# A four-layer transformer kernel on one core: the Fourier layer's residual tiles move to other homes and another queue, and the next layer's first weights are split earlier

## The chip, the core and the metric

The kernel runs on one core of a Trainium2 chip. A core has a matrix engine (PE, with its weight loads shown apart as PEld), a vector engine (DVE), an engine for functions of one input (ACT), a general engine (POOL) and a queue engine (SP) that mostly issues transfers. Each engine works through its own instructions in order and waits on semaphores of the others. Transfers between the chip's memory (HBM) and the on-core memory (SBUF) run on 16 DMA engines. They are issued here from two places: SP, whose transfers the profile lists as queue q1 ("hardware_dynamic"), and POOL, whose transfers are queue q0 ("software_dynamic").

The metric is the time of one execution in microseconds, as a median of several runs.

## What is computed

Four layers on x, a 2048 x 640 matrix of float32: attention, Fourier, attention, Fourier. Each is added to its input.

```python
def _A_ref(x, wqkv, wo):            # 32 heads of 20
    q, k, v = split((x @ wqkv))
    p = softmax(q k^T / sqrt(20))
    return (p @ v) @ wo

def _B_ref(x, dft_seq_re, dft_seq_im, dft_hid_re, dft_hid_im):
    a = x @ dft_hid_re^T
    b = x @ dft_hid_im^T
    return dft_seq_re @ a - dft_seq_im @ b

x = x + _A_ref(_layernorm(x), A_wqkv, A_wo)
x = x + _B_ref(_layernorm(x), ...)
x = x + _A_ref(_layernorm(x), A_wqkv, A_wo)
x = x + _B_ref(_layernorm(x), ...)
```

## The kernel before

The program has two equal halves, each of one attention layer and one Fourier layer. The first half writes its result to a buffer in HBM, `d_x[1]`; the second half reads it and writes the output.

**An attention layer** starts with a prologue (`prologue`, from line 284). For each of four blocks of 512 rows, PE turns the normalized rows (`turn`, tiles `xa` to `ptr`, split by ACT and DVE into two parts `xt`), makes the first 128 columns of the queries and of the keys (`pqk`, two times 15 matmuls with the weights `w[0]` and `w[1]`) and half of the values (`pv`, 60 matmuls). A float32 matrix is handled as the sum of a rounded part and a rest: ACT casts (line 114) and DVE subtracts (line 115). That is `split`; `weights` is a split of a weight tile `wraw` into `wqk`. The attention proper follows (`psc`, `e`, `acc`), then the projection with `wo` (`py`, class `Project`), which adds the residual, writes the sum to `d_x[0]` (line 960) and normalizes it into the tiles `xn`.

**A Fourier layer** (`Fourier.run`, line 1224) uses the symmetry of the transform: the rows are folded, so that row blocks are handled in eight pairs t = 0 to 7, pair t being blocks t and t + 8. Its main loop has 16 steps; step i handles block m = `ORDER[i]` of the sequence matrix. In a step PE adds 9 matmuls to the sums `pacc` (`accumulate`); after the last of a group of four steps ACT and DVE split the sums into the tiles `u` (`turn`), which frees the banks of PSUM that hold them; and `parts(i + 6)` splits the matrix block that is needed six steps later (`craw` to `chl`) and, after the second block of a pair, issues the load of a further 512 KB piece of the matrix into the freed `craw` slot (line 1119, on SP). The last three such loads are issued at steps 0, 1 and 3.

From step 11 on, `hidden(t)` makes pair t: 18 matmuls `phid`, one ACT copy and two DVE operations that make the sum and the difference `r` (lines 1190 to 1192), then the residual is added: DVE adds the lower block, POOL the upper (lines 1200 and 1201), two instructions each, and SP stores the tile `xd` to `d_x[1]` or to the output (line 1222). `hidden(0)` to `hidden(3)` run within the main loop; `hidden(4)` to `hidden(7)` after it.

**The residual tile** of a pair is 640 KB, loaded from `d_x[0]` by `residual(t)` (line 1197) on POOL's queue. Its home is one of six tiles `x0` to `x5` in the pool `own`. Pairs 0 to 3 are asked for at steps 2, 3, 5 and 7, pairs 4 and 5 at steps 8 and 9. Pairs 6 and 7 reuse the homes of pairs 0 and 1 and are asked for just ahead of `hidden(4)` and `hidden(5)`; since POOL also adds the upper blocks, these two requests stand between its additions.

**The passage to the next half.** `after(s)`, called ahead of `hidden(4)`, makes a `Start` of the next attention layer: ACT normalizes its first 512 rows out of the residual tiles of pairs 0 to 3, and SP asks for `wraw` and for `wvraw`. After `hidden(7)` and the release of the pools the prologue opens a pool `pro`, whose tiles `w0` and `w1` take the split weights, and loads rows 512 to 1023 (`xa`), which are the lower blocks of pairs 4 to 7.

The addresses follow from the pools. In the kernel before, the tile for `w[0]` lies on the addresses of the tile that is home to pairs 1 and 7.

```python
        def residual(s, t):
            s.x[t] = s.own(f"x{t % 6}", [2, D], F32, "xd")
            G.dma_start(s.x[t], pair(s.src, t))
```

Of the kernel before, what the change touches and what calls it, by code (L numbers as in the profile page):

```python
# [19 lines left out]
ND = D // 128  # L20
# [15 lines left out]
def mha_fnet_kernel(ctx, tc, x_in, wqk, wv, wo, seq, hid, nat_seq, nat_hid, out):  # L36
# [123 lines left out]
    class Qkv:  # L160
# [98 lines left out]
            else:  # L259
                A.activation(dst, src, AF.Copy)  # L260

        def begin(s, first, kq, vals, given):


            s.first, s.given = first, given
            for k in range(2):
                if given:
                    s.xn[k] = first(f"x{k}", [2, D], F32, "xa")
                    for i in range(2):
                        normed(s.xn[k][:, i], given.x[2 * k + i][:, 0], given.next[k], i)  # L270
                else:
                    s.load(k)
            s.fetch(0, kq, "k3")
            s.fetch(ND, kq, "k4")
            s.wvraw = [vals(f"v{NT - 1 - dc}", [HD], F32, "wvraw") for dc in range(ND)]
            if given:
                s.load_values()
# [2 lines left out]
            for dc in range(ND):  # L280
                nc.sync.dma_start(s.wvraw[dc], wv[dc, :, :HD])

        def prologue(s, vals, xt, fill, room, att):
            s.xtp, s.fill, s.room = xt, fill, room
            for k in (2, 3):
                s.load(k)
            if not s.given:
                s.load_values()
            s.top = const.tile([128, 2, ND, NB], F32, name="top", bufs=2)
            V.memset(s.top, 0.0)  # L290
            w = [room(f"w{k}", [2, ND, 128], F32R, "wqk") for k in range(2)]
            def values():
                s.wv = fill("wv", [ND, 2, HD], F32R, "wv")
                for dc in range(ND):
                    split(s.wv[:, dc, 0], s.wv[:, dc, 1], s.wvraw[dc])

            if s.given:
                s.weights(w[0], 0, False)
                s.turn(0)
                s.weights(w[1], ND, False)  # L300
                values()
            else:
                s.stats(0)
                s.norm(0)
                s.stats(1)
                for k in range(2):
                    s.weights(w[k], k * ND, False)
                s.norm(1)
                s.stats(2)
                s.turn(0)  # L310
                s.norm(2)
                s.stats(3)
                values()

            def ones(t):
                s.v[t] = vals(f"v{t}", [H * VW + 12], F32, "v")
                G.memset(s.v[t][:, :H * VW].rearrange("p (a c) -> p a c", c=VW)[:, :, DH:], 1.0)
                G.memset(s.v[t][:, H * VW:], 1.0)

            for t in range(NT - ND):  # L320
                ones(t)
            def later(tb, k, f):
                if tb + 2 < NB:
                    f(2 * tb + 4 + k)

            def own(tb, n):
                t = 4 * tb + n
                p = s.bank([128, HD], "pv")
                for dc in range(ND):
                    for f in s.value(p, t, dc):  # L330
                        f()
                s.own(p, t, 0, False)

            for tb in range(NB):

                sq, late = [], s.given and tb == 0
                for k in range(2):
                    later(tb, k, s.load)
                for k in range(2):
                    p = s.bank([128, 512], "pqk")  # L340
                    for dc in range(ND):
                        for f in s.product(p, w[k], tb, dc):
                            f()
                    sq.append(s.keep(p, k * ND, tb, False, (room, fill)[k]))
                    if late:
                        s.stats(2 + k)
                        continue
                    if tb == k == 0:
                        s.norm(3)
                    later(tb, k, s.stats)  # L350
                if late:
                    for n in range(4):
                        own(tb, n)
                        if n < 2:
                            s.norm(2 + n)
                            later(tb, n, s.stats)
                if tb == 0:
                    att.setup()
                elif tb == 1:
                    for t in range(NT - ND, NT):  # L360
                        ones(t)
                if tb + 1 < NB:
                    s.turn(tb + 1)
                for k in range(2):
                    later(tb, k, s.norm)
                    s.norms(s.bank([H, 512], "pn"), k * ND, tb, sq[k])
                if tb == 0:
                    att.qload(0, 0, None)
                elif tb == 1:
                    s.fetch(ND + 1)  # L370
                    for j in range(2):
                        att.kload(0, 0, j)
                elif tb == 2:
                    s.w1 = s.weights(s.fill("w", [2, ND, 128], F32R, "wqk"), ND + 1, True)
                    s.fetch(1)
                elif tb == NB - 1:
                    att.zeros(room)
                    list(s.bound(0, room))
                    att.qshift(0, 0)
                    for j in range(2):  # L380
                        att.kload(0, 1, j)
                if not late:
                    for n in range(4):
                        own(tb, n)
            s.made |= {0, ND}
# [656 lines left out]
    class Fourier:  # L1042
# [68 lines left out]
        ORDER = (0, 1, 4, 5, 2, 6, 3, 7) + tuple(range(8, 16))  # L1111
        AHEAD = 6

        def load(s, slot):

            if s.loads:
                n = s.loads.pop(0)
                s.raw[n] = s.keep(f"raw{slot}", [2, 512], F32, "craw"), slot
                nc.sync.dma_start(s.raw[n][0], seq[n // 4, n // 2 % 2, FIRST[n % 2 * 2] // 2])
# [73 lines left out]
            return r  # L1193

        def residual(s, t):
            s.x[t] = s.own(f"x{t % 6}", [2, D], F32, "xd")
            G.dma_start(s.x[t], pair(s.src, t))

        def add(s, e, x, r, r_mirror):
            e.tensor_tensor(x[:, :HD + 1], x[:, :HD + 1], r[:, :HD + 1], op=OP.add)  # L1200
# [2 lines left out]
        def hidden(s, t):  # L1203
# [8 lines left out]
            r = s.difference_and_sum(p, s.own(f"r{t % 2}", [3 * (HD + 2)], F32, "r"), 128)  # L1212
            if t in (0, 2):

                m = s.own("xs", [D], F32, "xs")[0:1]
                G.tensor_copy(m, hi[0:1])
                s.add(G, m, s.ym[:, t // 2], s.ym[:, 1 - t // 2])
            s.add(V, lo, r[:, 0], r[:, 1])
            s.add(G, hi, r[:, 1], r[:, 0])
            if t in (0, 2):  # L1220
                G.tensor_copy(hi[0:1], m)
# [2 lines left out]
        def run(s, after):  # L1224

            s.x, s.acc, s.nb, s.next = {}, {}, 0, {}
            for i, m in enumerate(s.ORDER):
                tb, ri, q = m // 8, (m // 4) % 2, m % 4
                s.accumulate(m)
                if q == NQ - 1:  # L1230
                    s.turn(tb, ri)
                s.parts(i + s.AHEAD)
                if m in (6, 7, 9, 10):
                    s.middle((6, 7, 9, 10).index(m))
                if 11 <= m < 14:
                    s.hidden(m - 11)
                if m == 13:
                    s.hidden(3)
                if m in (12, 13) and s.dst is not out:
                    k = m - 12  # L1240
                    s.next[k] = moments([s.x[2 * k + i][:, 0] for i in range(2)], 2, "a")
                if ri == 1 and m < 8:
                    s.residual(q)
                elif m in (8, 9):
                    s.residual(m - 4)
            s.keep.close()
            after(s)
            for t in range(4, NP):
                if t < 6:
                    s.residual(t + 2)  # L1250
                s.hidden(t)

        def general(s):

# [47 lines left out]
    class Start:  # L1302


        def __init__(s, L, src, general, given=None):
            s.tag = tag = f"{L}g" if general else f"{L}"
            s.q = Qkv(tag, src)
            s.q.flag = near[:, 5 + L:6 + L] if general else near[:, L:L + 1]
            s.a = Attention(s.q, tag)
            s.vals, s.a.kq, s.first = Pool(f"v{tag}"), Pool(f"kq{tag}"), Pool(f"first{tag}")  # L1310
            s.q.begin(s.first, s.a.kq, s.vals, given)

    def layer(start, src, dst, general, tasks, after):

# [2 lines left out]
        f = Fourier(p, d_x[0], dst, check)  # L1317
        f.tag = tag
        xt, fill = Pool(f"xt{tag}", "right"), Pool(f"fill{tag}", "right")
        room = Pool(f"pro{tag}")  # L1320
        banks(f"q{tag}")
        q.prologue(vals, xt, fill, room, a)
        room.close()
        start.first.close()

        room = a.room = check.room = Pool(f"att{tag}")
# [40 lines left out]
    def layers(general):  # L1367
        todo = [Start(0, x_in, general)]
        for L in range(LAYERS):
            last = L == LAYERS - 1  # L1370

            def after(f=None):
                if not last:
                    todo.append(Start(L + 1, d_x[1], general, f))

            layer(todo[L], d_x[1] if L else x_in, out if last else d_x[1], general, tasks[L], after)
            if general:
# [78 lines left out]
```

## Time and profile before

| | |
|---|---|
| time, median of 3 runs | 2580.6 us (2579.59 to 2583.07) |
| time of the profiled execution | 2582.69 us |
| its span, first to last instruction | 2580.8 us |
| PE busy | 2521.1 us, 98% |
| ACT busy | 2136.0 us, 83% |
| DVE busy | 981.2 us, 38% |
| POOL busy | 538.4 us, 21% |
| mean granted PE clock | 0.993 |
| first half's Fourier layer and passage, from the first `pacc` to the second half's first `pqk` at full pace | 1214.80 to 1298.65 us |
| second half's Fourier layer, from the first `pacc` to the last addition | 2497.42 to 2573.72 us |

The profiled execution is 2.1 us above the median of the runs and within their range. Its time is 1.9 us longer than its span. Shares over the whole span hide the Fourier layers, which are some 160 us of 2580; they have to be read with views cut to a stretch of time.

### The profile page before, as it was taken

The page shows a single profiled execution, that of the slowest core. Times are in us where ns is not written, and L with a number is a line of the kernel's source. Part 1 is how long each engine was busy: PE and PEld are TensorE (multiplying, and loading weights), DVE is VectorE, ACT ScalarE, POOL GpSimd, SP SyncE. Part 2 cuts the span into 40 slices and gives each one's busy share as a digit, 9 for nine tenths or more (in the row PEclk, how much of TensorE's full clock was granted, in tenths as well). Part 3 has the DMA queues.
Part 4 walks back from the last instruction along what each step waited for, and adds up shares of the span by engine and source line. Part 5 has one row for each costly group of instructions (what it writes and reads, how often), then busy time and mean ns, then how long its engine had stood idle before and what let it go on. Part 6 is the DMA issues. An engine that isn't in the chain of part 4 may idle for free.

```text
span 2580.8 us, 43627 instructions
## 1 busy us (share of the span) xinstructions
PE 2521.1 (98%) x16350; PEld 1161.6 (45%) x16350; DVE 981.2 (38%) x2081; ACT 2136.0 (83%) x2429; POOL 538.4 (21%) x1068
## 2 busy tenths in 40 slices
PE   8999999999999999999989999999999999999997
PEld 7644444443333332249775444444433333322596
DVE  5244422244232334317653444223332323332275
ACT  5688899988999999975356888999899999999752
POOL 2112111112111212114321211111111111121243
PEclk9999999999999999999999999999999999999998
DMA  5223221222322223336442332222221212133463
GB/s 175 95 91 122 83 86 44 85 88 85 94 70 87 87 81 109 123 96 236 181 164 93 105 119 89 66 65 72 84 83 51 80 51 77 52 94 97 131 245 130
DMA packets 124345, 262.53 MB, mean 102 GB/s; under 512 B 28016, under 2 KB 52368, under 8 KB 124124
## 3 DMA queue, kind: packets, MB, share of 16 engines
q1 hardware_dynamic: 83228, 149.30, 17.9%
q0 software_dynamic: 40896, 110.34, 13.5%
q8 instruction: 132, 2.16, 0.4%
q14 instruction: 89, 0.73, 0.1%
HBM read 175.29 MB, written 84.21 MB: 101 GB/s over the span
## 4 chain that ended last, share of the span: by engine, by line
PE 90%; DVE 4%; DMA 2%; POOL 1%; issue 1%; ACT 1%; DVEq 0%; SPq 0%; ACTq 0%; POOLq 0%
PE acc L534 37%; PE psc L523 27%; PE pqk L127 11%; PE pv L127 6%; PE py L120 2%; PE py L122 2%; PE py L121 2%; PE pn L227 1%; DVE of L541 1%; PE ptr L192 1%; DMA craw<-in_seq_dram 1%; DMA xd<-d_x 1%; PE pacc L120 0%; PE pacc L121 0%; PE pacc L122 0%
## 5 line engine op out<-in xcount | busy, mean ns | idle before, releaser
L526 ACT ACTIVATE e<-psc 128x1024 f32<-128x1024 f32 x2048 | 1937.9, 1118 | 163.0 <-PE psc L523 126.5
L534 PE MATMUL acc<-e,v 128*32 128x512 f32 x8192 | 1061.6, 602 | 3.8 <-DVE of L541 3.3
L523 PE MATMUL psc<-stq,stk 62*128 62x512 f32 x4096 | 816.5, 462 | 4.5 <-ACT e L526 3.0
L523 PEld LDWEIGHTS psc<-stq,stk 62*128 62x128 f32 x4096 | 341.9, 184 | 838.0 <-ACT e L526 789.4
L534 PEld LDWEIGHTS acc<-e,v 128*32 128x32 f32 x8192 | 187.6, 108 | 365.7 <-issue 338.1
L555 POOL DMA_DIRECT2D o<-oh x256 | 131.2, 521 | 991.2 <-DVE oh L550 989.9
L127 PE MATMUL pqk<-xt,wqk 128*128 128x512 f32 x1200 | 317.9, 409 | 14.4 <-ACT xt L114 8.8
L127 PEld LDWEIGHTS pqk<-xt,wqk 128*128 128x128 f32 x1200 | 217.5, 190 | 100.8 <-issue 37.0
L541 DVE STREAM_TRANSPOSE of<-acc 128x512 f32<-128x512 f32 x64 | 45.8, 716 | 532.0 <-PE acc L534 517.7
L112 DVE CAST hl<-pqk 128x512 fp32r<-128x512 f32 x64 | 44.2, 690 | 427.9 <-PE pqk L127 427.9
L127 PE MATMUL pv<-wv,xt 128*128 128x320 f32 x960 | 159.7, 317 | 0.0
L127 PEld LDWEIGHTS pv<-wv,xt 128*128 128x128 f32 x960 | 141.0, 188 | 25.6 <-issue 21.5
L555 POOL DMA_DIRECT2D o<-ot x256 | 128.3, 510 | 1.1 <-DMA o<-oh 0.3
L222 POOL DMA_DIRECT2D scrq<-hl x40 | 28.3, 708 | 394.2 <-DVE hl L115 264.1
L766 DVE TENSOR_REDUCE far<-cq 128x1 f32<-128x512 f32 (+5 forms) x169 | 98.5, 584 | 5.7
L120 PE MATMUL py<-wo,o 128*128 128x320 f32 x320 | 99.1, 310 | 1.4 <-DVE xr L948 1.4
L122 PE MATMUL py<-wo,o 128*128 128x320 f32 x320 | 98.7, 308 | 0.0
L121 PE MATMUL py<-wo,o 128*128 128x320 f32 x320 | 98.6, 308 | 0.0
L770 DVE TENSOR_TENSOR cq<-cq 128x512 f32<-128x512 f32 (+4 forms) x166 | 96.3, 580 | 2.8 <-DMA cq<-in_nat_seq_dram 2.7
L222 POOL DMA_DIRECT2D scrk<-hl x40 | 28.1, 702 | 294.3 <-DVE hl L115 248.5
L258 DVE COPY v<-pv 128x320 f32<-128x320 f32 x32 | 15.7, 489 | 183.8 <-PE pv L127 183.8
L228 DVE TENSOR_REDUCE top<-pn 32x1 f32<-32x512 f32 x80 | 53.4, 675 | 30.4 <-PE pn L227 30.4
(195 smaller groups left out, 1754.3 us busy)
## 6 DMA issues: line engine op xcount, KB each, us to landing
cq<-in_nat_seq_dram POOLq DMA_DIRECT2D x64, 512.0 KB, 5.3
scrq<-hl POOLq DMA_DIRECT2D x40, 512.0 KB, 3.2
scrk<-hl POOLq DMA_DIRECT2D x40, 512.0 KB, 3.5
stq<-scrq SPq DMA_DIRECT2D x256, 80.0 KB
stk<-scrk SPq DMA_DIRECT2D x128, 160.0 KB
o<-o SPq DMA_DIRECT2D x16, 1280.0 KB
stq<-scrq SPq DMA_DIRECT2D x256, 40.0 KB
stk<-scrk SPq DMA_DIRECT2D x128, 80.0 KB
```

The costliest lines, as they stand in the source:

```text
L120: PE.matmul(out_ap, ah, bh, start=start, stop=False)
L121: PE.matmul(out_ap, ah, bl, start=False, stop=False)
L122: PE.matmul(out_ap, al, bh, start=False, stop=stop)
L127: yield lambda i=i, j=j, k=k: PE.matmul(out_ap, a[i], b[j], start=dc == 0 and k == 0, stop=dc == ND - 1 and k == 2)
L222: G.dma_start(s.scr["qk"[k]][c * 128:(c + 1) * 128, :, tb * 512:(tb + 1) * 512], hl.bitcast(F32))
L523: PE.matmul(p[:, i], s.k[g, kc // 8, j][r, kc % 8 * 128:(kc % 8 + 1) * 128], s.q[g, qb, j][r], start=True, stop=True)
L526: A.activation(e, p, AF.Exp, scale=SCALE)
L534: PE.matmul(s.acc[32 * j:32 * j + 32], s.a.v[kc][:, v0:v0 + 32], s.e[n, j // 2][:, j % 2], start=kc == 0, stop=kc == NT - 1, skip_group_ch ...
L541: V.transpose(t0.rearrange("p b c -> p (b c)"), s.acc)
L555: G.dma_start(s.o[k, h * DH:(h + 1) * DH, qb * 512:(qb + 1) * 512], hl[k][32 * j:32 * j + DH])
L766: V.tensor_reduce(to, x, op=OP.max, axis=AX.X, apply_absolute_value=True)
L770: V.tensor_tensor(y, x, y, op=op)
```

## The change

Six things change, in both halves unless said otherwise.

1. The residual loads are issued by SP, no longer by POOL.
2. Their place: pairs 0 to 5 at steps 4 to 9, behind the last three loads of the matrix; pairs 6 and 7 at step 13, right after `hidden(3)`.
3. Their homes: pairs 0 to 4 lie in the five tiles of the projection's weights `wo`, pair 5 in a tile `x5` of its own, pairs 6 and 7 in `u2` and `u3`, whose old sums `hidden(3)` has read last. No home is used by two pairs.
4. The one-row tile `xs` moves to `raw0`; the tiles of the pool `own` are laid out in another order.
5. First half only: the pool `pro` of the next attention layer is opened with `Start`, and the split of its weights `w[0]` stands between `hidden(4)` and `hidden(5)`, that of `w[1]` between `hidden(5)` and `hidden(6)`.
6. First half only: for pair 7 POOL adds the lower block too, ahead of the upper one.

```diff
+        def early(s, k):
+            w = s.w[k] = s.room(f"w{k}", [2, ND, 128], F32R, "wqk")
+            s.weights(w, k * ND, False)
...
             if s.given:
-                s.weights(w[0], 0, False)
                 s.turn(0)
-                s.weights(w[1], ND, False)
                 values()
...
+        HOMES = [f"wo{t}" for t in range(ND)] + ["x5", "u2", "u3"]
...
         def residual(s, t):
-            s.x[t] = s.own(f"x{t % 6}", [2, D], F32, "xd")
-            G.dma_start(s.x[t], pair(s.src, t))
+            s.x[t] = (s.late if t < ND else s.own)(s.HOMES[t], [2, D], F32, "xd")
+            nc.sync.dma_start(s.x[t], pair(s.src, t))
...
-                m = s.own("xs", [D], F32, "xs")[0:1]
+                m = s.late("raw0", [D], F32, "xs")[0:1]
...
-            s.add(V, lo, r[:, 0], r[:, 1])
+            s.add(G if t == NP - 1 and s.dst is not out else V, lo, r[:, 0], r[:, 1])
             s.add(G, hi, r[:, 1], r[:, 0])
...
+            for tag, shape in [(f"r{k}", [3 * (HD + 2)]) for k in range(2)] + [("u2", [3, 512]), ("u3", [3, 512]),
+                                                                             ("x5", [2, D])]:
+                s.own(tag, shape, F32, "place")
...
                 if m == 13:
                     s.hidden(3)
+                    for t in (6, 7):
+                        s.residual(t)
...
-                if ri == 1 and m < 8:
-                    s.residual(q)
-                elif m in (8, 9):
-                    s.residual(m - 4)
+                if 4 <= i < 10:
+                    s.residual(i - 4)
             s.keep.close()
-            after(s)
+            begun = after(s)
             for t in range(4, NP):
-                if t < 6:
-                    s.residual(t + 2)
                 s.hidden(t)
+                if begun and t < 6:
+                    begun.q.early(t - 4)
```

On SP, in the first half from the projection's last stores to the second half's first loads. `xr` is the projection's sum, `xd` the residual tile, `wraw` and `wvraw` the next attention layer's raw weights, `xa` its rows. Before:

```order
L960 DMA d_x_87<-xr 128x2x640 x3
L1119 DMA craw<-in_seq_dram 128x1024 x3
L1222 DMA d_x_88<-xd 128x2x640 x4
L200 DMA wraw<-in_wqk_dram 128x640 x2
L281 DMA wvraw<-in_wv_dram 128x320 x5
L1222 DMA d_x_88<-xd 128x2x640 x4
L175 DMA xa<-d_x_88 128x2x640 x4
```

and changed:

```order
L963 DMA d_x_87<-xr 128x2x640 x3
L1124 DMA craw<-in_seq_dram 128x1024 x3
L1202 DMA xd<-d_x_87 128x2x640 x6
L1228 DMA d_x_88<-xd 128x2x640 x4
L1202 DMA xd<-d_x_87 128x2x640 x2
L200 DMA wraw<-in_wqk_dram 128x640 x2
L286 DMA wvraw<-in_wv_dram 128x320 x5
L1228 DMA d_x_88<-xd 128x2x640 x4
L175 DMA xa<-d_x_88 128x2x640 x4
```

Six residual loads now stand behind the three loads of the matrix, and two stand ahead of the weights.

On ACT, in the same half, from the normalizing of the next layer's first rows (`xa`) to the split of the value weights. Each `r` row is the ACT part of one `hidden`. Before:

```order
L154 ACTIVATE xa<-xd,ars 128x640 x4
L1190 ACTIVATE r<-phid 128x322 x4
L114 ACTIVATE wqk<-wraw 128x640
L114 ACTIVATE xt<-ptr 128x512 x5
L114 ACTIVATE wqk<-wraw 128x640
L114 ACTIVATE wv<-wvraw 128x320 x5
```

and changed:

```order
L154 ACTIVATE xa<-xd,ars 128x640 x4
L1195 ACTIVATE r<-phid 128x322
L114 ACTIVATE wqk<-wraw 128x640
L1195 ACTIVATE r<-phid 128x322
L114 ACTIVATE wqk<-wraw 128x640
L1195 ACTIVATE r<-phid 128x322 x2
L114 ACTIVATE xt<-ptr 128x512 x5
L114 ACTIVATE wv<-wvraw 128x320 x5
```

The two casts of weights moved from beside the turned rows `xt` to between the pairs; DVE's two subtractions moved in the same way. On POOL the eight requests for `xd` are gone, and pair 7 has four additions where it had two.

More of the change, by code (lines that the diff above doesn't have):

```diff
@@ L260, in own, with begin @@
                 A.activation(dst, src, AF.Copy)
-        def begin(s, first, kq, vals, given):
-            s.first, s.given = first, given
+        def early(s, k):
+            w = s.w[k] = s.room(f"w{k}", [2, ND, 128], F32R, "wqk")
+            s.weights(w, k * ND, False)
+        def begin(s, first, kq, vals, room, given):
+            s.first, s.room, s.given, s.w = first, room, given, {}
             for k in range(2):
@@ L281, in load_values, with prologue @@
                 nc.sync.dma_start(s.wvraw[dc], wv[dc, :, :HD])
-        def prologue(s, vals, xt, fill, room, att):
-            s.xtp, s.fill, s.room = xt, fill, room
+        def prologue(s, vals, xt, fill, att):
+            s.xtp, s.fill, room = xt, fill, s.room
             for k in (2, 3):
@@ L290, in prologue @@
             V.memset(s.top, 0.0)
-            w = [room(f"w{k}", [2, ND, 128], F32R, "wqk") for k in range(2)]
             def values():
@@ L306, in prologue @@
                 for k in range(2):
-                    s.weights(w[k], k * ND, False)
+                    s.early(k)
                 s.norm(1)
@@ L341, in prologue @@
                     for dc in range(ND):
-                        for f in s.product(p, w[k], tb, dc):
+                        for f in s.product(p, s.w[k], tb, dc):
                             f()
@@ L1309, in __init__ @@
             s.a = Attention(s.q, tag)
-            s.vals, s.a.kq, s.first = Pool(f"v{tag}"), Pool(f"kq{tag}"), Pool(f"first{tag}")
-            s.q.begin(s.first, s.a.kq, s.vals, given)
+            s.vals, s.a.kq, s.first, s.room = [Pool(n + tag) for n in ("v", "kq", "first", "pro")]
+            s.q.begin(s.first, s.a.kq, s.vals, s.room, given)
     def layer(start, src, dst, general, tasks, after):
@@ L1319, in layer @@
         xt, fill = Pool(f"xt{tag}", "right"), Pool(f"fill{tag}", "right")
-        room = Pool(f"pro{tag}")
         banks(f"q{tag}")
-        q.prologue(vals, xt, fill, room, a)
-        room.close()
+        q.prologue(vals, xt, fill, a)
+        start.room.close()
         start.first.close()
@@ L1374, in after @@
                     todo.append(Start(L + 1, d_x[1], general, f))
+                    return todo[-1]
             layer(todo[L], d_x[1] if L else x_in, out if last else d_x[1], general, tasks[L], after)
```

## Prediction

> **What bounds the kernel now.** I read the page's totals and the chain of waits first; then the chain cut to the Fourier layers, PE's timeline there, and the DMA traffic by stretch.
>
> ```profile
> PE 2521.1 (98%) x16350; PEld 1161.6 (45%) x16350; DVE 981.2 (38%) x2081; ACT 2136.0 (83%) x2429; POOL 538.4 (21%) x1068
> ...
> PE 90%; DVE 4%; DMA 2%; POOL 1%; issue 1%; ACT 1%; DVEq 0%; SPq 0%; ACTq 0%; POOLq 0%
> ```
>
> PE sets the pace nearly everywhere, and the change takes no matmul away. It can gain only where PE waits, or where the granted clock is low after a wait. The chain in the first half's Fourier layer (start, length, what) shows one such place:
>
> ```profile
> 1227.88 8.00 DMA craw<-in_seq_dram
> 1235.96 0.64 ACT chl L114
> ...
> 1238.57 0.79 PE pacc L120
> ```
>
> A piece of the sequence matrix takes 8.00 us to land. Behind its split, in order on ACT and DVE, stands the split `u` of the finished sums, which frees PE's banks. PE's timeline there, and the same place in the second half:
>
> ```profile
> 1238.57 0.79 PE L120 MATMUL pacc<-chl,xn 128*128 128x512 f32 x1 [2.95 <-DVE u L115]
> 1239.16 0.63 PE L121 MATMUL pacc<-chl,xn 128*128 128x512 f32 x1
> ...
> 1244.71 0.43 PE L122 MATMUL pacc<-chl,xn 128*128 128x512 f32 x1
> 1244.98 0.40 PE L120 MATMUL pacc<-chl,xn 128*65 128x512 f32 x1
> 1245.22 0.39 PE L121 MATMUL pacc<-chl,xn 128*65 128x512 f32 x1
> ...
> 2522.40 0.80 PE L120 MATMUL pacc<-chl,xn 128*128 128x512 f32 x1 [3.46 <-DVE u L115]
> 2523.00 0.63 PE L121 MATMUL pacc<-chl,xn 128*128 128x512 f32 x1
> ...
> 2528.12 0.45 PE L121 MATMUL pacc<-chl,xn 128*128 128x512 f32 x1
> ```
>
> PE idles 2.95 us, and then 13 matmuls start 0.427 us apart ((1244.71 - 1239.16) / 13) where the warm ones start 0.24 apart: the clock is down after the wait. The second half shows 3.46 us and 12 such distances. Why does the piece take 8 us? The DMA queues in three stretches, 1228 to 1231, 1231 to 1236 and 1236 to 1238:
>
> ```profile
> q0 software_dynamic: 262, 1.18, 101.0%
> ...
> q0 software_dynamic: 253, 1.16, 60.0%
> q1 hardware_dynamic: 220, 0.84, 41.9%
> ...
> q1 hardware_dynamic: 199, 0.70, 88.5%
> ```
>
> For 3 us after the request all 16 engines serve q0, POOL's six residual loads; then the two queues share. The residuals are in the matrix's way.
>
> The second place is the passage to the next half (chain, then PE):
>
> ```profile
> 1282.40 8.38 DMA xd<-d_x
> ...
> 1293.05 3.12 DMA d_x<-xd
> ...
> 1296.40 0.74 ACT wqk L114
> ...
> 1297.99 0.61 DVE xt L115
> ...
> 1298.65 8.83 PE pqk L127 x29
> ...
> 1316.27 2.18 PE ptr L192 x20
> ...
> 1318.99 7.03 PE pqk L127 x30
> ...
> 1286.50 2.40 PE L192 MATMUL ptr<-ident,xa 128*128 128x128 f32 x20 [0.67 <-ACT r L1190]
> ```
>
> Pair 7's residual is asked for at 1282.40, lands at 1290.8, is added and stored; only when the store has landed (1296.2) does ACT cast `wqk`, whose tile lies on that residual's home. ACT's and DVE's next entries, the turned rows, stand behind it. PE has next to nothing from 1288.9 to 1298.65, and then runs 29 `pqk` in 8.83 us where 30 take 7.03.
>
> **The change, part by part.** Durations are the profiled execution's (2582.7 us).
>
> *Matrix ahead of residuals, both halves.* The pieces are asked for when they were (the wait is for DVE's split that frees the slot), but no residual is under way. What they then take:
>
> ```profile
> 1274.07 1.91 SPq L1222 DMA_DIRECT2D d_x<-xd  x2
> ...
> GB/s 0 0 0 0 90 397 410 397 384 397 371 358 358 397 410 410 397 397 358 320 243 218 179 166 346 397 384 397 371 384 410 378 378 365 339 77 77 128 154 109
> ```
>
> The second row is the traffic from 1274 to 1282 in steps of 0.2 us: a store issued on idle queues moves bytes 0.7 us later, at about 0.39 MB per us. 640 KB take 1.7 us so, and the store above, 3.12 in all, leaves 0.7 for completion; 512 KB take 1.3. So the first piece would land 2.8 us after its request; I take 3.2, as two more are asked for while it moves: 1231.1, 4.9 us sooner. From its landing to PE's restart the chain needs 2.6 us (1235.96 to 1238.57), which gives 1233.7, ahead of PE's need at 1238.57 - 2.95 = 1235.6. The stall goes, with 1.9 us to spare. First half: 2.95 + 13 x (0.427 - 0.24) = 5.4 us. Second: 3.46 + 12 x 0.187 = 5.7. Bounds: nothing, if the pieces land as late as now; 5.8 and 6.1, if the first slow distance (0.59 and 0.60) counts too. I take 5.4 and 5.7, being nearest to the idle-queue rows.
>
> Late next are the six residuals: 1.6 + 3.9 MB at 0.39 MB per us end near 1243. The first addition,
>
> ```profile
> 1258.48 0.49 DVE L1200 TENSOR_TENSOR xd<-xd,r 128x321 f32<-128x321 f32 x1
> ```
>
> moves to 1253 with the gain: covered by 10 us. On SP nothing else waits behind them until pair 0's store. POOL loses eight issues of 0.75 us that hid in its idle time: nothing.
>
> *Passage, first half* (in the trace's own clock, without the shift of 5.4 us). The rows that price it:
>
> ```profile
> 1278.96 0.42 ACT L1190 ACTIVATE r<-phid 128x322 f32<-128x322 f32 x1
> ...
> 1282.85 2.24 DVE L1201 TENSOR_TENSOR xd<-xd,r 128x319 f32<-128x319 f32 x1
> ...
> 1285.01 0.48 DVE L1191 TENSOR_TENSOR r<-phid,r 128x322 f32<-128x322 f32 x1
> ...
> 1287.28 0.48 DVE L1191 TENSOR_TENSOR r<-phid,r 128x322 f32<-128x322 f32 x1
> ...
> 1297.17 0.82 DVE L115 TENSOR_TENSOR wqk<-wraw,wqk 128x640 fp32r<-128x640 f32 x1 [4.81 <-ACT wqk L114]
> ...
> 1274.02 0.74 POOL L1200 TENSOR_TENSOR xd<-xd,r 128x321 f32<-128x321 f32 x1
> 1274.72 0.88 POOL L1201 TENSOR_TENSOR xd<-xd,r 128x319 f32<-128x319 f32 x1
> ...
> 1313.09 1.74 ACT L154 ACTIVATE xa<-xa,ars 128x640 f32<-128x640 f32 x2 [0.75 <-DVE ast L145]
> ```
>
> The weights' home no longer touches a residual, so the old wait goes. A new one takes part of it: on SP the weights stand behind the loads of pairs 6 and 7. From 1274.75 on, two stores, these two loads (655 KB each) and the first weight tile (328 KB) are 2.95 MB, or 7.6 us: it lands near 1283. ACT is free for its cast at 1279.4 and must wait, with the `r` of pairs 5 to 7 and then the turned rows queued behind. PE does not feel that at once: pairs 4 to 7 write eight different banks. From 1283 ACT needs 0.74 for the cast, and DVE then does split 0.82, pair 5 in 2.27 (start to start above), split 0.82, pair 6 in 2.27, pair 7's `r` in 0.97 and the first turned rows in 0.61: 7.8 us, to about 1291.5. PE starts `pqk` there instead of at 1298.65: 7.2 us. With a shorter idle time before it (some 2 us, then the turning, then 1 us) I count half of the slow clock's 2.0 us (8.83 against 29/30 of 7.03) as saved: **8.2 us**. Bounds: 11.2, if the weights are there at once (DVE from 1279.4 + 2.27 = 1281.7) and the clock stays up; 4.4, if each of the two splits takes DVE's worst 2.24 and the clock stays low.
>
> The Trainium skill ("TensorE: Matmul & The Clock Gate", Part 1) has the clock halved after an idle window of about 3.4 us; in the rows above 2.95 already did it. By its figure these gaps would cost nothing and the gain be 1 us larger.
>
> The Trainium skill ("DMA: Bandwidth & Descriptors", Queues, rings and completion order) says that each DMA engine takes turns between queues and keeps ring order within one. The shared stretch from 1231 agrees, the first 3 us do not. It speaks against this part of the change: on one queue the weights cannot pass the two residuals, where on two they would share. By it the wait above stands in full; without it, the gain would be nearer 11.
>
> *Pair 7 on POOL.* DVE is spared 1.3 us (2.27 less 0.97) just ahead of the turned rows, which is counted above; POOL pays 0.74 + 0.88 more, and only the store behind it waits for that (first rival).
>
> *End of the second half.* The residual of pair 7 is late here too:
>
> ```profile
> 2564.62 6.86 DMA xd<-d_x
> ...
> 2571.62 1.05 POOL xd L1200
> ...
> 2570.26 0.48 DVE L1192 TENSOR_TENSOR r<-phid,r 128x322 f32<-128x322 f32 x1
> ```
>
> `r` is done at 2570.74 and the addition starts at 2571.62: **0.9 us** to gain and no more, as the store behind it stays.
>
> Sum: 5.4 + 5.7 + 8.2 + 0.9 = 20.2 us. 2582.7 - 20.2 = 2562.5 for such an execution. The profiled one is 2.1 above the median of 2580.6, so I predict 2560 for the median.
>
> **Rivals.**
>
> *The passage hands its gain on.* Before the next turning (1316.27) rows 512 to 1023 must be stored, loaded, measured and normalized. Pair 7's `r` at 1290.9, four POOL additions 3.2, the store 3.1 with 0.2 to issue, the load as much again, statistics up to the normalizing
>
> ```profile
> 1309.24 0.88 DVE L145 BATCH_NORM_STATS2 ast<-xa 128x6 f32<-128x320 f32 x2
> ```
>
> 3.85 (1309.24 to 1313.09) and the normalizing 1.74 give 1306.2; PE arrives after `pqk` and `pv` at 1291.5 + 7.8 + 8.8 = 1308.1. The margin is 1.9 us, against 1.4 now (1314.83 to 1316.27). If the load takes 8.4 us as pair 7's residual did, PE waits 3.4 us and loses clock for 2: 20.2 - 5.4, or 15 us in all, 2565. For it: the value weights and four stores share the queue. Against: most of them are over by then.
>
> *The front stays.* Should another wait, such as the sums' own split, keep PE idle as long, only 8.2 + 0.9 remain: 2571.5. Against: the chain shows no second releaser within 3 us.
>
> *Slower: the residuals still run against the matrix.* They are issued on the same queue 0.4 us apart, right behind it. If the DMA engines served everything outstanding alike, the first piece would finish with the last: 5.5 MB, 14 us, near 1242 instead of 1236. PE would lose 6 us more in each half, 12 in all, against the 9.1 gained elsewhere: 2583.5. It decides from a landing at 8 + 9.1 / 2 = 12.5 us. Against: the three pieces of now. The first had landed at 1235.96 when only 0.84 of the 1.57 MB had moved, so it was served ahead of the others.
>
> *The change does nothing that counts*: the waits move to neighbours one for one, 2580.
>
> **How the numbers follow.** Forecast 0.72; handed on 0.13; front stays 0.08; slower 0.03; nothing 0.04. The forecast's own range is 2580.6 less 24.0 (5.8 + 6.1 + 11.2 + 0.9) to less 16.4 (5.4 + 5.7 + 4.4 + 0.9): 2556 to 2564. For 8 in 10 and more I reach up to the third case and, for what the four parts may gain together, a little down: 2553 to 2571. A measurement of this kernel tells 0.2%, 5 us, from no change. Faster by more: 0.93; within: 0.04; slower: 0.03.
>
> **What would show it.** Right: a `craw` landing of 3 to 4 us at the three loads; no gap of PE ahead of the ninth block of sums in either half; `wqk` cast between the `r` rows, ACT idle there for some 3 us on the DMA of `wraw`; the next half's `pqk` about 13 us sooner (5.4 from the front among them); no wait for `xd` at the end. Wrong: a new idle time of PE at the second turning, or a landing of `craw` that stays at 8 us.

## The result, and the profile after

| | before | changed |
|---|---|---|
| median of 6 runs | 2580.47 us (2579.59 to 2583.07) | 2562.99 us (2561.14 to 2564.92) |
| profiled execution | 2582.69 us | 2562.02 us |
| its span | 2580.8 us | 2560.2 us |

The ratio is 0.9931, with a 95% interval of 0.9918 to 0.9944: 17.5 us faster. The forecast was 2560, with a range of 2553 to 2571. Two executions on record stand apart by their granted clock: one of the kernel with the fronts alone (3309.56 us at 0.654), which is left out of its figures below, and one of the kernel before in the last group (2603.66 us at 0.944), which widens the intervals of that group. The page's totals of the changed kernel and its chain by engine stand nearly as they stood:

```profile
PE 2511.1 (98%) x16350; PEld 1156.3 (45%) x16350; DVE 978.0 (38%) x2079; ACT 2136.1 (83%) x2429; POOL 527.8 (21%) x1054
...
PE 90%; DVE 4%; DMA 2%; POOL 1%; issue 1%; ACT 1%; SPq 0%; DVEq 0%; ACTq 0%; POOLq 0%
```

PE is as bound as before, and its busy time fell by 10.0 us although it has the same 16350 matmuls: fewer of them run at the low clock (mean granted clock 0.997, where it was 0.993).

**The fronts.** SP's rows of the changed kernel, and ACT's timeline at the place where ACT had stood 8.04 us (start, length, engine, line, operation; in brackets the idle time ahead and what ended it):

```profile
1225.77 2.13 SPq L1124 DMA_DIRECT2D craw<-in_seq_dram  x3
1227.99 3.34 SPq L1202 DMA_DIRECT2D xd<-d_x  x6
```

```profile
1229.24 1.15 ACT L114 ACTIVATE chl<-craw 128x512 fp32r<-128x512 f32 x2 [2.88 <-DMA craw<-in_seq_dram]
1230.49 1.56 ACT L114 ACTIVATE u<-pacc 128x512 fp32r<-128x512 f32 x3
```

The first matrix piece is asked for at 1225.77 and can be split at 1229.24, 3.5 us later, where it took 8.0. Traffic by queue from 1228 to 1231, the stretch in which q0 had all engines before, now has one queue only:

```profile
q1 hardware_dynamic: 279, 1.01, 94.8%
```

PE shows no idle time ahead of the ninth block of sums, in either half, and the clock stays up. It reaches the twelve small matmuls `pturn`, two blocks further on, here (before, changed):

```profile
1245.77 1.28 PE L1173 MATMUL pturn<-one,c3raw 1*128 1x1 f32 x12
...
2529.41 1.28 PE L1173 MATMUL pturn<-one,c3raw 1*128 1x1 f32 x12
```

```profile
1238.17 1.28 PE L1178 MATMUL pturn<-one,c3raw 1*128 1x1 f32 x12
...
2509.71 1.28 PE L1178 MATMUL pturn<-one,c3raw 1*128 1x1 f32 x12
```

**The passage.** ACT's and PE's timelines of the changed kernel:

```profile
1271.29 0.42 ACT L1195 ACTIVATE r<-phid 128x322 f32<-128x322 f32 x1
1277.66 0.74 ACT L114 ACTIVATE wqk<-wraw 128x640 fp32r<-128x640 f32 x1 [5.95 <-DMA wraw<-in_wqk_dram]
1278.30 0.42 ACT L1195 ACTIVATE r<-phid 128x322 f32<-128x322 f32 x1
...
1282.16 0.44 ACT L1195 ACTIVATE r<-phid 128x322 f32<-128x322 f32 x1 [2.48 <-POOL xd L1206]
```

```profile
1282.65 4.32 PE L192 MATMUL ptr<-ident,xa 128*128 128x128 f32 x20 [4.53 <-ACT r L1195]
1286.73 7.11 PE L127 MATMUL pqk<-xt,wqk 128*128 128x512 f32 x30
...
1324.65 7.00 PE L127 MATMUL pqk<-xt,wqk 128*128 128x512 f32 x30
```

and PE's of the kernel before, for the same products and for the third group of them:

```profile
1297.67 0.79 PE L127 MATMUL pqk<-xt,wqk 128*128 128x512 f32 x1 [8.77 <-ACT xt L114]
...
1337.57 7.00 PE L127 MATMUL pqk<-xt,wqk 128*128 128x512 f32 x30
```

The 8.77 us between turning and products are gone. But the wait that the prediction announced has come, and is longer: ACT stands 5.95 us on the weights, and PE then stands 4.53 us ahead of the turning, where it had stood 0.67.

To compare kernels I use four intervals between the same instructions of PE in the profiled executions: the **first front**, from the first `pacc` to `pturn`; the **passage**, from there to the next half's third group of 30 `pqk` (the row at 1324.65 above), so that what is given back in the prologue counts too; the **second front**; and the **end**, from the second half's `pturn` to the last addition. They leave out what varies from run to run in the attention layers.

| | first front | passage | second front | end |
|---|---|---|---|---|
| before | 31.67 | 91.80 | 31.99 | 44.31 |
| changed | 25.63 | 86.48 | 25.63 | 43.23 |
| gained | 6.0 | 5.3 | 6.4 | 1.1 |

Together 18.8 us. The two spans differ by 20.6; the rest, 1.8 us, stands nearly all ahead of the first `pacc`, where the change moves nothing. That `pacc` starts at 1214.10 before and at 1212.54 changed; the 1214.80 in the table of the kernel before is the fourth one. The passage of the changed kernel came out at 86.48 here and at 86.59 when the kernel was run again, so differences of a few tenths are not read.

### The profile page after: what moved, and what is told of

Same layout as the page of the kernel before. It is cut to its first block, busy times and chain, and to the rows that moved or that the text cites. A ratio compares the mean times of both kernels' runs of the same rounds, so it can differ in the third digit from the quotient of the medians.

```text
span 2560.2 us, 43615 instructions
## 1 busy us (share of the span) xinstructions
PE 2511.1 (98%) x16350; PEld 1156.3 (45%) x16350; DVE 978.0 (38%) x2079; ACT 2136.1 (83%) x2429; POOL 527.8 (21%) x1054
## 3 DMA queue, kind: packets, MB, share of 16 engines
q1 hardware_dynamic: 87580, 159.79, 18.8%
## 4 chain that ended last, share of the span: by engine, by line
PE 90%; DVE 4%; DMA 2%; POOL 1%; issue 1%; ACT 1%; SPq 0%; DVEq 0%; ACTq 0%; POOLq 0%
PE acc L537 37%; PE psc L526 27%; PE pqk L127 10%; PE pv L127 5%; PE py L120 2%; PE py L122 2%; PE py L121 2%; PE pacc L120 1%; PE pacc L121 1%; PE pacc L122 1%; PE pn L227 1%; DVE of L544 1%; PE ptr L192 0%; DMA xa<-d_x 0%; POOL o L558 0%
```

## Experiments

The theory after the comparison: the fronts are gained by the queue on which the residuals are asked for, not by their place in the program; and in the passage the new homes gain some 10 us, of which the early split of the weights gives half back, because its first piece is late. Each run below undoes or adds one part. The time of the kernel before on the chips of the three groups was 2579.8, 2578.9 and 2581.1.

### The residuals back on POOL's queue, in their new place

```diff
-            nc.sync.dma_start(s.x[t], pair(s.src, t))
+            (G if t < 6 else nc.sync).dma_start(s.x[t], pair(s.src, t))
```

> The changed kernel with one thing undone: the residual loads of pairs 0 to 5 are issued by POOL again, from the new place (steps 4 to 9) and into the new homes. Theory A, the queue is what counts: POOL has no other work ahead of its request there, so it asks as early as before (some 6 us ahead of the matrix pieces), the pieces take about 8 us to land again, PE idles about 3 us in each half with some 13 slow matmuls behind it, and the 5.9 and 6.4 us that the changed kernel shows at the two fronts are gone: about 2563 + 12 = 2575 us. Theory B, the place in the program is what counts: the loads stand behind the matrix in the text, so pieces land in 3.5 us and the time stays at 2563.

Measured: 2574.96 us, ratio 0.9981 (0.9972 to 0.9991). First front 29.99, passage 86.65, second front 32.19. POOL's and PE's timelines of this kernel:

```profile
1221.65 4.46 POOL L1202 DMA_DIRECT2D xd<-d_x  x6 [0.42 <-issue]
```

```profile
1238.81 0.50 PE L120 MATMUL pacc<-chl,xn 128*128 128x512 f32 x1 [3.16 <-DVE u L115]
1239.15 0.40 PE L121 MATMUL pacc<-chl,xn 128*128 128x512 f32 x1
...
2515.37 0.80 PE L120 MATMUL pacc<-chl,xn 128*128 128x512 f32 x1 [3.87 <-DVE u L115]
```

The requests stand behind the matrix loads in the program, but on another engine. POOL has nothing to wait for and issues them at 1221.65, 6 us ahead of the matrix loads, which SP issues when their slots are free:

```profile
1227.88 2.13 SPq L1124 DMA_DIRECT2D craw<-in_seq_dram  x3
```

Both stalls are back and the passage is unchanged. A place in the program ordered these transfers only where one queue issued both. No run asks for the residuals on SP at the old steps, so the queue is shown to be needed, not to be enough by itself.

### The fronts alone, on the kernel before

```diff
-            G.dma_start(s.x[t], pair(s.src, t))
+            (nc.sync if t < 6 else G).dma_start(s.x[t], pair(s.src, t))
...
-                if ri == 1 and m < 8:
-                    s.residual(q)
-                elif m in (8, 9):
-                    s.residual(m - 4)
+                if 4 <= i < 10:
+                    s.residual(i - 4)
```

> The kernel before with one part of the change: the residual loads of pairs 0 to 5 are issued by SP at steps 4 to 9, into the old homes x0 to x5; pairs 6 and 7, the weights' split and everything else stay as before. Theory A, the front's gain is kept to the end: 5.9 + 6.4 = 12.3 us, 2580.5 - 12.3 = 2568. Theory B, the passage is bound by its own chain of transfers and gives part of it back: 2571 to 2575. If the new homes were needed for the front, pieces would land late here: 2580.

Measured: 2569.2 us (median of four, 2567.29 to 2571.14), ratio 0.996 (0.9944 to 0.9976). Both fronts 25.63, as in the changed kernel; passage 90.68, 1.1 us shorter than before. The fronts need only this part: 6.0 and 6.4 us without new homes or an early split. PE in the passage of this kernel:

```profile
1282.10 2.40 PE L192 MATMUL ptr<-ident,xa 128*128 128x128 f32 x20 [0.67 <-ACT r L1190]
1292.44 0.80 PE L127 MATMUL pqk<-xt,wqk 128*128 128x512 f32 x1 [7.94 <-ACT xt L114]
```

The old wait between turning and products stays.

### The early split undone in the changed kernel

```diff
             if s.given:
+                s.early(0)
                 s.turn(0)
+                s.early(1)
                 values()
...
-                if begun and t < 6:
-                    begun.q.early(t - 4)
```

> The changed kernel without the early split: w[0] is split just ahead of the first turned rows and w[1] behind them, as before; the loads of pairs 6 and 7, the homes and POOL's additions stay changed. In the changed kernel ACT waits 5.95 us in its order for the first weight tile, with the last pairs' work and the turned rows behind it. Theory A, that wait is what keeps the passage's gain at 5 us: without it pairs 5 to 7 run at PE's pace, the weights (landed by then) cost one cast and one subtraction (1.6 us), and the first matmuls of the next layer start 3 to 5 us sooner: 2558 to 2560. Theory B, the early split is what brings the passage's gain: the start moves back by the two splits and the time rises by 2 to 4 us: 2565 to 2567.

Measured: 2558.6 us, ratio 0.9918 (0.9901 to 0.9935), 4.4 us below the changed kernel's median. Passage 81.40: 10.4 us shorter than before, 5.1 shorter than in the changed kernel. PE in the passage:

```profile
1281.30 2.40 PE L192 MATMUL ptr<-ident,xa 128*128 128x128 f32 x20 [0.67 <-ACT r L1197]
1283.46 7.48 PE L127 MATMUL pqk<-xt,wqk 128*128 128x512 f32 x30
```

Turning and products follow each other at the full clock. So the old wait goes without the early split, and the part of the change that was to fill the passage better costs half of what the others bring. Which others is not taken apart: this kernel keeps the new homes, the earlier requests for pairs 6 and 7 that these homes allow, and POOL's additions for pair 7. The kernel with the fronts alone, which has none of the three, has a passage of 90.68; from there they are worth 9.3 us together.

### The weights asked for ahead of the last two residuals

```diff
                 if m == 13:
                     s.hidden(3)
-                    for t in (6, 7):
-                        s.residual(t)
...
             begun = after(s)
+            for t in (6, 7):
+                s.residual(t)
```

> The changed kernel with the loads of pairs 6 and 7 behind the requests for the weights and value weights on SP (just ahead of pair 4's sums), everything else as changed. Theory A, the queue serves roughly in order: 1.31 MB less ahead of the first weight tile, at 0.38 MB per us, lets it land 3.4 us sooner; ACT's wait falls from 5.95 to about 2.5 us and the next layer starts about 3 us sooner: 2560. Theory B, all that is outstanding shares: the landing moves by less than 1 us and the time stays at 2563. If pair 6's residual is late instead, DVE and POOL wait for it and the time stays or rises.

Measured: 2559.58 us, ratio 0.9925 (0.9908 to 0.9941). Passage 83.83. ACT's timeline:

```profile
1272.01 0.74 ACT L114 ACTIVATE wqk<-wraw 128x640 fp32r<-128x640 f32 x1 [0.89 <-DMA wraw<-in_wqk_dram]
...
1284.89 1.92 ACT L114 ACTIVATE wv<-wvraw 128x320 fp32r<-128x320 f32 x5 [3.35 <-POOL v L320]
```

The wait on the weights falls from 5.95 to 0.89 us, so the piece comes 5.1 us sooner where 3.4 was expected for 1.31 MB less ahead of it, and the passage is 2.7 us shorter. That is less than the 5.1 above although the piece is nearly in time: not all of the early split's cost is lateness.

### All eight residuals behind the matrix, with and without the early split

Pairs 6 and 7 get tiles of their own and are asked for with the others, so that nothing but the stores stands ahead of the weights:

```diff
-        HOMES = [f"wo{t}" for t in range(ND)] + ["x5", "u2", "u3"]
+        HOMES = [f"wo{t}" for t in range(ND)] + ["x5", "x6", "x7"]
...
-                    for t in (6, 7):
-                        s.residual(t)
...
-                    s.residual(i - 4)
+                    for t in range(i - 4, i - 3 if i < 9 else NP):
+                        s.residual(t)
```

The rooms for the split weights and for the rest of the prologue become two pools, which makes space. The second kernel also undoes the early split, as above.

> All eight residuals are requested behind the matrix, at the six places where six were; pairs 6 and 7 lie in tiles of their own, and nothing but the two stores stands on the queue ahead of the next layer's first weights, which are still split among the last sums. Theory A (in the changed kernel the passage gains 5.3 to 5.7 us and not 8.2, because the first weight piece lands 7.47 us after its issue, behind two stores and two residuals, and ScalarE stands 5.95 us with pair 7's work behind it): the piece lands within 4 us of its issue, ScalarE's wait on it falls below 3 us, the rows of pair 7 are turned earlier, the first products begin 4 to 6 us sooner than in the changed kernel, and the time falls to 2557 to 2560, part of it lost again at the next waits of that stage (the last residual 'r' and the loads of the stored rows). Rival (the piece is slow by itself, since the value weights share the stretch with it): the landing stays at 6 us or more, the wait at 4 us or more, and the time at 2562 to 2564. Rival of the front: two more residuals behind the matrix hold back the third, smaller matrix piece and TensorE stops again at the ninth block of sums: 2566 or more.

> As the kernel with all eight residuals behind the matrix, and the split of the first weights is put back where it was, after the last rows of the half and around the first turning. Theory A (the early split costs only because its piece is late): with the eight residuals behind the matrix it no longer matters where the split stands, and this kernel and the one with the early split come out within 2 us of each other, both at 2557 to 2560. Rival (the early split costs by its own work: 0.75 us of ScalarE and 1.5 us of VectorE twice, ahead of pair 7's rows, whatever the piece's landing): this one is 2 to 4 us below the other. Rival (two residuals ahead of the weights cost nothing once the split is late): this one equals the kernel that only puts the split back, 2558.6.

Measured with the early split: 2559.97 us, ratio 0.9921 (0.9903 to 0.994), passage 82.98. Without it: 2557.44 us, ratio 0.9913 (0.9896 to 0.993), passage 81.27. ACT and PE with the early split:

```profile
1272.58 0.74 ACT L114 ACTIVATE wqk<-wraw 128x640 fp32r<-128x640 f32 x1 [0.92 <-DMA wraw<-in_wqk_dram]
...
1278.35 0.44 ACT L1195 ACTIVATE r<-phid 128x322 f32<-128x322 f32 x1 [2.31 <-POOL xd L1206]
```

```profile
1281.00 0.48 PE L127 MATMUL pqk<-xt,wqk 128*128 128x512 f32 x1
1282.64 6.85 PE L127 MATMUL pqk<-xt,wqk 128*128 128x512 f32 x29 [1.16 <-DVE xt L115]
```

and PE without it:

```profile
1278.77 2.40 PE L192 MATMUL ptr<-ident,xa 128*128 128x128 f32 x20 [0.67 <-ACT r L1197]
1280.93 7.50 PE L127 MATMUL pqk<-xt,wqk 128*128 128x512 f32 x30
```

Three things follow from the four passages (86.48 changed, 82.98 all eight, 81.40 late split, 81.27 both). With the two residuals out of the way the piece lands 4.2 us after its issue at 1268.39, not 7.5, and the passage is 3.5 us shorter: that much of the early split's cost was lateness. Another 1.7 us goes when the split moves back, with the piece in time: that is its own work on ACT and DVE ahead of pair 7's, and PE's wait of 1.16 for DVE's turned rows, which the other kernel does not have, shows most of it. And with the split late the two residuals cost nothing (81.40 against 81.27), so the place of those two matters only through the early split. Of the three expectations for the second kernel, the one that the split costs by its own work fits (2.5 us in the medians, 1.7 in the passage, its lower edge or just below); the first, that the two come out within 2 us, is not ruled out by the passage, and it is PE's wait that speaks against it; and the one that it equals the kernel with the late split alone fits too, as far as 1.2 us between two groups of runs can tell.

### Pair 7's lower addition back on DVE

```diff
-            s.add(G if t == NP - 1 and s.dst is not out else V, lo, r[:, 0], r[:, 1])
+            s.add(V, lo, r[:, 0], r[:, 1])
```

> The changed kernel with pair 7's lower addition back on VectorE. Prediction's step (the additions on VectorE, 1.3 us more than the turned rows that stand behind them can spare, delay the next half's first products): the first turned copies come 1 to 1.3 us later and the time is 2564. Theory A (in the changed kernel VectorE is not what ends the wait there: the turning waits for ScalarE's 'r', behind the late weight piece, and the store of pair 7 is sooner by POOL's 1.6 us): no change, 2562 to 2563, or up to 1.5 us faster where the store of the last rows decides what follows.

Measured: 2563.72 us (2561.75 to 2564.9), ratio 0.9936 (0.9919 to 0.9954); passage 86.74, against 86.48. Counted from `pturn`, the first values `pv` come 1.0 us later than in the changed kernel, not 1.3 (56.49 against 55.50), and the next groups take that up again. Nothing of it reaches the end that these runs can tell.

### The best kernel beside the changed one

> The changed kernel itself, on the same chip as the one below and in turn with it, so that the two can be compared directly. Theory A: 2563, 17 us below the kernel before, as in its first runs.

> The kernel with all eight residuals behind the matrix and the first weights split after the last rows, on the same chip and in turn with the changed kernel. Theory A: the 5.5 us that the late weight piece still costs in the changed kernel are gained, 2557 to 2558, and the two ranges of times don't overlap. Rival (the difference of 5 us seen between two chips' runs was the chip's): within 2 us of the changed kernel.

Measured in turn on one chip: changed 2563.07 us (2561.74 to 2564.73), ratio 0.9925 (0.9896 to 0.9954); all eight residuals behind the matrix and the late split 2557.1 us (2555.3 to 2559.63), ratio 0.9902 (0.9873 to 0.9932). The ranges of times don't overlap: 6.0 us between the medians, with passages of 86.59 and 80.98. The last kernel beats both the kernel before and the changed one.

## Why the prediction came out as it did

**What bounds the kernel** was read rightly: the time came from PE's waits and the slow clock behind them, at the two places named.

**Fronts, 5.4 and 5.7 predicted, 6.0 and 6.4 measured.** The step is right as it was put: the piece landed after 3.5 us (3.2 taken), PE has no gap, and the fronts come alone when only that part is done. The terms were a little small. They took the stall and the thirteen slow distances; the first slow matmul, kept as the upper bound (5.8 and 6.1), should have been in the sum.

**Passage, 8.2 predicted, 5.3 measured.** This is the mis-sized term, and it fails at one step: "it lands near 1283". In the changed kernel's time that is 1275.4 (7.6 us less, the shift at `pturn`); ACT could begin its cast at 1277.66, 2.3 us later, and stood 5.95 us instead of 3.6 (1279.4 to 1283). The sum of bytes ahead, as I made it, ended at the piece's own last byte. With only the stores ahead it holds. SP's rows of the kernel with all eight residuals behind the matrix:

```profile
1266.39 1.90 SPq L1228 DMA_DIRECT2D d_x<-xd  x2
1268.39 1.58 SPq L200 DMA_DIRECT2D wraw<-in_wqk_dram  x2
```

Bytes move from 1267.1, 0.7 after the first store's issue; two stores and the piece are 1.64 MB, 4.2 us at 0.39 MB per us, and 0.7 for completion gives 1272.0. Measured: 1272.58. With the two residuals ahead it does not hold; the changed kernel's chain has the piece under way for 7.47 us:

```profile
1270.17 7.47 DMA wraw<-in_wqk_dram
...
1277.66 0.75 ACT wqk L114
...
1282.65 1.13 PE ptr L192 x4
```

From the first byte at 1267.1 to 0.7 before that landing, at 1276.94, the queue of the changed kernel moved

```profile
q1 hardware_dynamic: 1593, 3.52, 98.4%
```

3.52 MB, 0.57 more than the 2.95 of the sum. So bytes of later requests moved beside the piece, worth 1.5 us at 0.39 MB per us. The other 0.8 us is the rate: 3.52 MB in 9.84 us are 0.36 per us, with a dip around 1270.7, behind the two stores, in the changed kernel and in the one with all eight residuals ahead (half a microsecond of each, the last number in GB/s):

```profile
1270.50:1271.00 0.50, 0.50 (x6) 0.50 (x5) 0.00 (x0) 0.50 (x2) 0.00 (x0) 1.00 0.92 184
...
1270.50:1271.00 0.50, 0.50 (x6) 0.50 (x5) 0.00 (x0) 0.50 (x2) 0.00 (x0) 1.00 0.92 179
```

The traffic row in the prediction has the same dip, and the sum took 0.39 throughout. Whose the 0.57 MB were is not shown: the piece's other half and the value weights stood next on the queue, and no run kept the two residuals and took the value weights away.

From the cast to `pqk` the chain took 9.1 us (1277.66 to 1286.73) where 8.5 was reckoned (1283 to 1291.5): DVE's second split took 1.47 us and not 0.82,

```profile
1281.34 1.47 DVE L115 TENSOR_TENSOR wqk<-wraw,wqk 128x640 fp32r<-128x640 f32 x1
```

which the lower bound, with 2.24, had held possible. On the other side the clock gave 1 us more than counted: 30 `pqk` in 7.11 are at full speed, so all of the 2.0 us of slow products were saved, not half. The turning ahead of them ran slowly instead (20 `ptr` in 4.32 against 2.40), beside DVE's work, and the clock was up again at 1286.6, when `pqk` began. At the first `pv` the passage had gained 6.0 us (13.64 between the kernels at that row, less 7.60 at `pturn`); 0.7 is given back until the third block. That is the first rival, the gain handed on, at 0.7 us where I had priced it at 5.4; two small waits of PE at the values show a part of it:

```profile
1315.30 2.46 PE L127 MATMUL pv<-wv,xt 128*128 128x320 f32 x15 [0.17 <-DVE hl L220]
1317.95 6.86 PE L127 MATMUL pv<-wv,xt 128*128 128x320 f32 x45 [0.19 <-DVE xt L115]
```

What the sum missed altogether is which part earns it. It treated the homes and the early split as one edit with one price; the runs take them apart: all but the early split 10.4, the early split minus 5.1, of that 3.5 by lateness and 1.6 or 1.7 by its own work. That the 10.4 lies near the bound of 11.2, "if the weights are there at once", is chance: the bound was for weights split early. The material was in the prediction: it had PE waiting for splits that stand ahead of pair 5 and pair 6, and it never reckoned the other order.

**Pair 7 on POOL**, 1.3 us counted within the 8.2: 1.0 seen at the first values, nothing at the end.

**End, 0.9 predicted, 1.1 measured**; the last additions of the changed kernel wait for `r` and no longer for the residual.

**The total.** 20.2 predicted, 18.8 measured between the marks, 17.5 between the medians. The three terms that were too small by 1.5 us together make up for half of the one that was too large by 2.9; that is luck, and it flatters the total. The forecast of 2560 was 3 us low, and the measured 2563 lies inside the forecast's own range of 2556 to 2564.

**The rivals.** That the front stays: no gap, out. That residuals share the engines with the matrix: the landing of 3.5 us, far from the deciding 12.5, is against it; the matrix pieces, issued first on the same queue, went first. That waits move one for one: out in the fronts; in the passage a new wait did take the place of the old one, and took half.

## What to carry to other kernels

Order two transfers by issuing them on one queue: the same requests in the same place of the program, on another engine's queue, ran 6 us ahead and cost 11 us. Work pulled ahead into an in-order engine brings its own wait along: ask when its data lands, and which instructions stand behind it there, before asking how long it takes. Where a change frees a wait and also moves work into the freed time, price the two apart; here all that freed the wait was worth 10.4 us and the moved work minus 5.1.

## What the runs showed of the hardware

**A stall of one length halves the clock in one run and not in another.** PE's granted clock by microsecond at the first front, in the kernel before and in the kernel with the residuals back on POOL (stretch, sum of busy time and groups by engine PE, PEld, DVE, ACT, POOL, then the clock, DMA share and GB/s):

```profile
1237.00:1238.00 1.00, 0.00 (x0) 0.00 (x0) 1.00 (x3) 1.00 (x4) 0.00 (x0) 0.98 0.85 338
1238.00:1239.00 1.00, 0.43 (x1) 0.43 (x2) 1.00 (x2) 0.87 (x3) 0.00 (x0) 0.50 0.06 25
...
1244.00:1245.00 1.00, 1.00 (x5) 0.71 (x4) 0.73 (x2) 0.00 (x0) 0.00 (x0) 0.60 0.00 0
```

```profile
1238.00:1239.00 1.00, 0.19 (x1) 0.19 (x2) 1.00 (x3) 1.00 (x3) 0.00 (x0) 1.00 0.06 25
```

A gap of 2.95 us halved the clock; one of 3.16 us at the same place left it at 1.00. That is why undoing the queue lost 4.4 us in the first front and 6.6 in the second, where its gap of 3.87 did halve the clock. In the passage of the changed kernel the clock fell 1.7 us after PE's last matmul:

```profile
1279.00:1280.00 1.00, 0.00 (x0) 0.00 (x0) 1.00 (x4) 0.68 (x2) 0.00 (x0) 0.90 0.96 379
...
1286.00:1287.00 1.00, 1.00 (x7) 1.00 (x6) 1.00 (x3) 0.71 (x2) 1.00 (x2) 0.69 0.38 154
```

The clock shown is 1.00 or 0.50 but for single stretches between, so a mean says when it changed: 0.98 and 0.60 put the low stretch of the kernel before at 1237.96 to 1244.8, 0.90 and 0.69 that of the changed kernel at 1279.8 to 1286.6. Both last 6.8 us. The Trainium skill ("TensorE: Matmul & The Clock Gate", Part 1) has the clock set by a free-running window of 3413 ns, and lowered after an idle one. That the window runs on by itself agrees: in the kernel before the clock changes at 1237.96, 1244.8, 1292.6, 1302.8, 2521.4 and 2528.2, and each is a whole number of steps of 3.41 us from the first (2, 16, 19, 376 and 378). That a whole window must be idle does not agree, since 2.95 us sufficed.

What tells the two gaps apart is where a step falls in them. The gap of 2.95 us began at 1235.62, so 2.3 us of it lay in the window that closed at 1237.96. With POOL's queue the clock falls at 1288.46 in the passage; 15 steps back, a window closed at 1237.26 and cut the gap (1235.65 to 1238.81) into 1.6 and 1.55 us. In the changed kernel's passage 1.7 us before the close at 1279.8 sufficed. So in these runs the idle time within one window decided, and the edge lies between 1.6 and 1.7 us; as the profile models the ends of matmuls, that is an estimate.

**Turn-taking between queues is not there at once.** In the kernel before, and again in the kernel with POOL's queue, the matrix pieces of the other queue moved nothing for 3 us after their request. The two stretches, 1228 to 1231 and 1231 to 1236, in the latter kernel:

```profile
q0 software_dynamic: 259, 1.17, 100.8%
...
q0 software_dynamic: 234, 1.03, 53.9%
q1 hardware_dynamic: 249, 0.95, 47.5%
```

The Trainium skill ("DMA: Bandwidth & Descriptors", Queues, rings and completion order) has each engine change queues after a packet of some 9 to 17 descriptors. In the next 5 us the two queues did share evenly (q0 53.9% and q1 47.5% from 1231 to 1236), as it says; the first 3 us don't agree, and no run here shows why.
